# Products of v stored once and split when loaded, and the third slice's rounded weights kept in their tiles

## The chip, the cores and the metric

The kernel runs on one core of a Trainium2 chip. The core has four engines that matter here, each with its own queue of instructions worked off in order: TensorE (PE in the rows, with PEld for its weight loads), VectorE (DVE), ScalarE (ACT) and GpSimd (POOL); SP is a queue that only issues transfers, and GpSimd issues transfers too. What counts is the device time of one execution in microseconds (us), as the median of timed runs.

## The reference, cut to what matters

```
scores = einsum('bhij,hg->bgij', scale * q @ k.T, w_pre)   # heads mixed; 4 batches, 12 heads, 448 x 448
attn   = softmax(scores)
attn   = einsum('bhij,hg->bgij', attn, w_post)             # heads mixed again
x      = (attn @ v)  as [1792 tokens, 768]
h      = x @ w_in                                          # 768 -> 2048
out    = (max(h, 0) + alpha * min(h, 0)) @ w_out           # 2048 -> 768
```

All inputs of the second layer but alpha are drawn as 64-bit floats; w_in and w_out reach the chip so and are rounded to 32 bits there, with integer operations on VectorE (seven instructions for one half of a slice, see below).

## The kernel before

**Attention stage.** Work is cut into 16 chunks (4 batches, each with 120, 120, 120 and 90 queries) and these into groups of ten queries; two groups make one of 90 steps m. Per chunk: `qk` (L320, score products) and `qk_out` (L333, copies from PSUM into `st`, on ScalarE or VectorE); per group `relay` (L340, a transfer from `st` to `sr` that brings heads of one query side by side, RAHEAD = 3 steps early); per step `mix` (L347, first head mixing into `m`), `rmax` (L352, row maximum `nm` on VectorE), `exp` (L359, ScalarE), `norm` (L365 to L369, VectorE), `post` (L381, second head mixing into `pa`, 112 small matmuls) and `post_out` (L393, copies into `at`, on either engine). When a chunk is through, `pv` (L403) makes its products with v, x, in two halves hx; `pv_out` (L417, L419) splits each in a high part, rounded to TensorE's single-pass 32-bit type, and the low rest x - high; `store_x` (L424) stores both parts in HBM, in two transfers.

**Second stage.** x lies there as 4 blocks of 448 tokens (one batch each) and d_ff as 16 slices f of 128. A unit u is one block with one slice; the 64 units run in five groups of slices ([0,1,2], [3,4,5,6], [7,8,9], [10,11,12], [13,14,15]), within each over the blocks, forwards and backwards in turn. Of a unit, `l1` (L616) makes h = x w_in with 18 matmuls (high-high, high-low, low-high for six parts of 128), `act` (L629 to L635: t on ScalarE and VectorE, its high and low part g) the activation, and `l2` (L654) adds g w_out into six accumulators with 18 matmuls. TensorE's order is l1(u), l2(u-1), l1(u+1), ... After the last slice of a group the sums are taken out (`ao`, L664, L666). Three blocks of x lie in SBUF at a time; `prefetch` loads the next, six times in all, both parts (L518).

**Weights.** One half of a slice is w_in or w_out of one f. It is fetched (`cr`), rounded by seven VectorE operations (L60 to L68, the result in tile `ct`, of which there are two) and split into its high part on ScalarE (L546) and its low part on VectorE (L548), in tile `w`. The first three slices (NPRE = 3) are rounded during the attention stage, stored in HBM (`store_w`, L458), loaded again near its end (`load_pre`, L555) and split there. The other thirteen are rounded in the second stage by `convert2`, a generator that gives out one operation at a time against a budget: `conv_ops(0.8)` in the middle of a unit's activation and `conv_ops(3.4)` (0.6 after a group's last slice) at its end, a credit that runs up to 4.0 at most. Where the next unit's slice isn't ready, these lines force it ahead of l1:

```
while conv_at <= units[u][2] and units[u][2] >= NPRE:
    conv_ops(0.95)
l1(u)
```

**What sets the order.** Up to unit 1, `plan` sets it: a list of operations with engines, costs, due times (prio), predecessors and buffers (acq, rel), from which it takes at each moment the one that can start first, by start and due time; where an operation may run on ScalarE or VectorE it chooses. The names there are Q, S, L, M, R, E, N, P, A for the chain above, V, XH, XL, W for v's products, F, C, WS, LW, HH, HL for the weights, LX for x's loads, U and G for the first two units. Behind unit 1 the loop at the end of the kernel sets the order.

Of the kernel before, what the change touches and what calls it, by code (L numbers as in the profile page):

```python
# [21 lines left out]
NT = B * S  # L22
# [48 lines left out]
def plan(groups, first, chunk_list):  # L71
# [55 lines left out]
    for ci, (b, c) in enumerate(chunk_list):  # L127
        lb = (first[ci + 1] - 1) // 2
        mine = [("A",) + divmod(n, 2) for n in range(first[ci], first[ci + 1])]
        for hx in range(2):  # L130
# [3 lines left out]
            op(("XH", ci, hx), [act(0.8), dve(0.78)], pr, [("V", ci, hx)], (("xe", (ci, hx)),))  # L134
            op(("XL", ci, hx), dve(0.78), pr, [("XH", ci, hx)], rel=(("slot", (ci, hx, "v")),))
            for i in range(2):
                op(("W", ci, hx, i), dma(0.7), pr + 1, [("XL", ci, hx)], rel=(("xe", (ci, hx)),))
    nh = 2 * NPRE
    for i in range(nh):
# [8 lines left out]
        for k in range(2):  # L148
            op(("WS", i, k), dma(0.8), pr + 10 + k, [("C", i, 6)], rel=(("ct", i),))
    for bl in range(2):  # L150
        for i in range(2 * NCC):
            pr = NB - 10 + 6 * bl + i // 2
            op(("LX", bl, i), dma(0.95, 5.0), pr, [("LX", bl, -1), ("M", min(pr, NB - 1))])
        op(("LX", bl, -1), dma(0.0, 0.0), NB - 10 + 6 * bl, [("Q", NC - 1, 0)], (("st", ("x", bl)),))
    op(("OPEN",), dma(0.0, 0.0), NB - 9, [("Q", NC - 1, NP - 1), ("S", NC - 1, NP - 1)])
    for f in range(NPRE):
        for k in range(NWP):
            op(("LW", f, k), dma(0.8, 5.0), NB - 12 + 2 * f + k / 2, [("LW", f, -1)])
        op(("LW", f, -1), dma(0.0, 0.0), NB - 12 + 2 * f, [("WS", i, j) for i in range(nh) for j in range(2)], (("cr", ("w", f)),))
        for x in range(2):  # L160
            pr = NB - 3 + 1.2 * f + 0.6 * x
            before = [("OPEN",), ("V", NC - 2, 1)] + ([("HL", f, x - 1)] if x else [("HL", f - 1, 1)] if f else [])
            op(("HH", f, x), act(0.84), pr, [("LW", f, k) for k in range(NWP)] + before)
            op(("HL", f, x), dve(0.95), pr, [("HH", f, x)], rel=(("cr", ("w", f)),) if x else ())
    for u in range(2):
        op(("U", u), pe("U", "u"), NB + 2.5 + 2 * u, [("HL", u, 1), ("M", NB - 1)] + [("LX", 0, i) for i in range(2 * NCC)] + ([("V", NC - 1, 1)] if u else []),
# [58 lines left out]
def talking_heads_prelu(ctx: ExitStack, tc: tile.TileContext, q, k, v, w_pre, w_post, mask, w_in, w_out, alpha, out):  # L225
# [16 lines left out]
    x2 = dpool.tile([2, NCC, 128, NT], F32, name="x2")  # L242
    wsc = dpool.tile([NPRE, 128, 2 * DM], F32, name="wsc")
# [165 lines left out]
    def pv_out(ci, hx, part, eng):  # L409
        cn = CHUNKS[chunk_list[ci][1]][1]  # L410
        if part == 0:
            xe_t[ci, hx] = xep.tile([128, 2, 3, CW], F32R, tag="xe", name=f"xe{ci}_{hx}")
        xe, ps = xe_t[ci, hx], u_t["pv", ci, hx]
        hi, lo = (xe[:, i, :, :cn].rearrange("p c (k g) -> p c g k", k=GI) for i in range(2))
        src = ps[:, 0, :3 * CW].rearrange("p (c i) -> p c i", c=3)[:, :, :cn].rearrange("p c (g k) -> p c g k", k=GI)
        if part == 0:
# [4 lines left out]
    def store_x(ci, hx, i):  # L421
        b, c = chunk_list[ci]
        c0, cn = CHUNKS[c]
        nc.sync.dma_start(  # L424
            out=x2[i, 3 * hx:3 * hx + 3, :, b * S + c0:b * S + c0 + cn].rearrange("c p i -> p c i"),
            in_=xe_t[ci, hx][:, i, :, :cn].bitcast(F32))
# [33 lines left out]
    with tc.manual_schedule():  # L460
# [54 lines left out]
        def load_x(bl, i):  # L515
            open_x(bl, i)
            for t in range(2):
                nc.sync.dma_start(out=x_t[bl][:, t], in_=x2[t, :, :, bl * S:(bl + 1) * S].rearrange("c p i -> p c i"))  # L518

        def load_xp(bl, i, slot):  # L520
            if i < 0:
                open_x(bl, slot)
                return
            c, t = divmod(i, 2)
            nc.sync.dma_start(out=x_t[bl][:, t, c], in_=x2[t, c, :, bl * S:(bl + 1) * S])
# [148 lines left out]
        def split_pre(f, x, part):  # L674
            if x == 0 and part == 0:
                w_tile(f)
            split_w(f, x, wr[f][:, x * DM:(x + 1) * DM], part)
# [28 lines left out]
        def emit(n, e, got):  # L706
# [7 lines left out]
            elif kind in ("S", "A", "XH", "XL"):  # L714
# [108 lines left out]
```

## Time and profile before

| | |
|---|---|
| median of the timed runs | 854.63 us (853.2 to 855.88, 3 runs) |
| the profiled execution | 850.37 us, of which 848.6 us span |
| granted clock of TensorE, mean | 0.991 |
| busy: TensorE, weight loads, VectorE, ScalarE, GpSimd | 808.8, 665.0, 575.5, 341.3, 129.8 us |
| moved by DMA | 125.39 MB, mean 148 GB/s |

Busy time is the time in which an engine has an instruction running; the span runs from the first to the last instruction. A wait is told as the engine, the line that waited, the engine and line that ended the wait ("issue": nothing that the profile shows ended it), the total, the number and the longest. The attention stage ends at about 364 us, where unit 0 begins.

### The profile page before, as it was taken

How to read it: one execution, taken by the hardware profiler on the slowest of the kernel's cores; microseconds unless marked ns; L12 is line 12 of the kernel's file. 1: busy time of each engine (PE TensorE's matmuls, PEld its weight loads, DVE VectorE, ACT ScalarE, POOL GpSimd, SP SyncE). 2: the span in 40 equal slices, each digit the busy share in tenths (PEclk: the TensorE clock that was granted, in tenths of full speed). 3: DMA queues.
4: the chain of work that ended last, by engine and by line, in shares of the span. 5: the costliest groups of instructions: out<-in, count | busy, mean ns of one | idle time of the engine just before them, and what ended most of it. 6: DMA issues, size and time to landing. Idle time of an engine off the chain costs nothing.

```text
span 848.6 us, 24016 instructions
## 1 busy us (share of the span) xinstructions
PE 808.8 (95%) x10380; PEld 665.0 (78%) x10380; DVE 575.5 (68%) x1027; ACT 341.3 (40%) x715; POOL 129.8 (15%) x237
## 2 busy tenths in 40 slices
PE   8788998999898999889999999999999999999998
PEld 3455675677666777689999999989999899999997
DVE  5669787999697978675666877248773967763323
ACT  4657766776566775532322221112212212121111
POOL 4443324343242221000000000000000000000000
PEclk9999999999999999999999999999999999999999
DMA  8698878887897679777221431002510242104113
GB/s 214 185 205 253 222 205 215 238 241 219 208 241 204 205 220 283 235 188 284 75 75 37 148 133 40 36 0 84 196 46 29 74 168 75 38 1 172 48 48 124
DMA packets 75374, 125.39 MB, mean 148 GB/s; under 512 B 33876, under 2 KB 64020, under 8 KB 75268
## 3 DMA queue, kind: packets, MB, share of 16 engines
q1 hardware_dynamic: 58228, 64.78, 25.1%
q0 software_dynamic: 16560, 58.01, 24.0%
q8 instruction: 82, 1.34, 0.7%
q10 hardware_dynamic: 480, 1.06, 0.5%
q14 instruction: 24, 0.20, 0.1%
HBM read 66.16 MB, written 18.92 MB: 100 GB/s over the span
## 4 chain that ended last, share of the span: by engine, by line
PE 87%; DMA 5%; DVE 4%; issue 2%; ACT 2%; SPq 0%; POOL 0%; ACTq 0%; DVEq 0%
PE acc L654 27%; PE h L616 27%; PE x L403 9%; PE pa L381 9%; PE m L347 7%; PE s L320 7%; DMA cr<-in_w_in_dram 2%; DMA sr<-st 1%; ACT e L359 1%; DVE nm L352 1%; DMA k<-in_k_dram 1%; DVE at L393 1%; DMA x<-xe 1%; DMA q<-in_q_dram 0%; DVE ao L666 0%
## 5 line engine op out<-in xcount | busy, mean ns | idle before, releaser
L654 PE MATMUL acc<-g,w 128*128 128x448 f32 x1152 | 245.7, 366 | 3.3 <-DVE g L635 2.0
L616 PE MATMUL h<-x,w 128*128 128x448 f32 x1152 | 248.3, 368 | 0.0
L654 PEld LDWEIGHTS acc<-g,w 128*128 128x128 f32 x1152 | 216.0, 188 | 23.3 <-DVE g L635 2.8
L616 PEld LDWEIGHTS h<-x,w 128*128 128x128 f32 x1152 | 216.1, 188 | 21.2
L381 PEld LDWEIGHTS pa<-r,e 64*64 64x64 f32 x5040 | 107.3, 134 | 57.5 <-issue 36.1
L631 DVE SCALAR_TENSOR_TENSOR t<-t,oma,h 128x448 f32<-128x448 f32 x64 | 43.5, 680 | 156.7 <-ACT t L629 156.7
L629 ACT ACTIVATE t<-h 128x448 f32<-128x448 f32 x64 | 34.9, 545 | 271.3 <-PE h L616 271.3
L381 PE MATMUL pa<-r,e 64*64 64x60 f32 x5040 | 108.7, 221 | 18.5 <-issue 13.2
L359 ACT ACTIVATE e<-m,nm 128x448 f32<-128x448 f32 x180 | 113.3, 641 | 23.6 <-DVE nm L352 13.5
L352 DVE TENSOR_REDUCE nm<-m 128x2 f32<-128x896 f32 x90 | 97.3, 1085 | 14.6 <-PE m L347 14.0
L320 PE MATMUL s<-k,q 64*64 64x448 f32 (+2 forms) x768 | 96.7, 556 | 4.8 <-ACT e L359 1.5
L347 PE MATMUL m<-sr,wk 64*64 64x448 f32 x720 | 93.4, 560 | 6.0 <-DMA sr<-st 3.6
L403 PEld LDWEIGHTS x<-at,v 128*64 128x64 f32 x1536 | 77.6, 141 | 19.8 <-ACT e L359 5.8
L403 PE MATMUL x<-at,v 128*64 128x120 f32 (+1 forms) x1536 | 84.5, 268 | 2.2 <-DVE s L366 0.8
L340 POOL DMA_DIRECT2D sr<-st x90 | 54.9, 611 | 200.8 <-PE m L347 148.6
L393 ACT COPY at<-pa 128x480 f32<-128x480 f32 x95 | 53.8, 575 | 53.4 <-PE pa L381 50.8
L333 ACT COPY st<-s 120x896 f32<-120x896 f32 (+1 forms) x68 | 61.5, 912 | 27.8 <-PE s L320 24.3
L393 DVE COPY at<-pa 128x480 f32<-128x480 f32 x85 | 55.0, 652 | 17.9 <-PE pa L381 16.3
L633 ACT CAST g<-t 128x448 fp32r<-128x448 f32 x64 | 36.3, 567 | 51.1 <-DVE t L631 51.1
L666 DVE TENSOR_TENSOR ao<-ao,acc 128x448 f32<-128x448 f32 x96 | 52.7, 613 | 1.7 <-PE acc L654 1.7
L320 PEld LDWEIGHTS s<-k,q 64*64 64x64 f32 (+2 forms) x768 | 29.9, 131 | 28.8 <-issue 10.4
L635 DVE TENSOR_TENSOR g<-t,g 128x448 fp32r<-128x448 f32 x64 | 39.8, 622 | 16.2 <-ACT g L633 16.2
(51 smaller groups left out, 523.3 us busy)
## 6 DMA issues: line engine op xcount, KB each, us to landing
sr<-st SPq DMA_DIRECT2D x90, 210.0 KB
sr<-st POOLq DMA_DIRECT2D x90, 210.0 KB, 5.5
x<-x SPq DMA_DIRECT2D x12, 1344.0 KB
cr<-in_w_in_dram POOLq DMA_DIRECT2D x13, 768.0 KB, 4.7
cr<-in_w_out_dram POOLq DMA_DIRECT2D x13, 768.0 KB, 4.5
x<-xe SPq DMA_DIRECT2D x48, 180.0 KB
x<-x SPq DMA_DIRECT2D x24, 224.0 KB
out_dram<-ao SPq DMA_DIRECT2D x24, 224.0 KB
```

The source lines that it names most:

```text
L320: nc.tensor.matmul(ps[i0:i1, hf, :S], q_t[ci][r, p * cn + i0:p * cn + i1], k_t[b, p // 2][r, p % 2, :], start=True, stop=True)
L333: copy(dst[:cn, p], u_t.pop(("qk", ci, p))[:cn, :, :S])
L340: dma.dma_start(out=sr_t[n][SR0:SR0 + GP], in_=s_t[ci][r:CHUNKS[chunk_list[ci][1]][1]:CHUNKS[chunk_list[ci][1]][1] // GI])
L347: nc.tensor.matmul(ps[hf:hf + 64, u, :S], wk[r, :], g[r, :], start=True, stop=True)
L352: nc.vector.tensor_reduce(out=nm, in_=m_t[m][:, :, :S], axis=AX.X, op=ALU.max, negate=True)
L359: nc.scalar.activation(out=e_t[m][:, u], in_=m_t[m][:, u, :S], func=AF.Exp, bias=nm_t[m][:, u:u + 1], scale=1.0, accum_out=se_t[m][:, u:u ...
L381: nc.tensor.matmul(dst[:, :, HI * u:HI * u + HI], e[h, u, 64 * jb:64 * jb + 64], r[h, u].rearrange("p (h i) -> p h i", h=H), start=True, s ...
L393: copy_on[eng](dst, pa[g][:, :NS * GP].rearrange("p (s i) -> p s i", i=GI))
L403: nc.tensor.matmul(ps[64 * t:64 * t + 64, 0, cl * CW:cl * CW + cn], v_t[b, hx][:, s, (2 * cl + t) * D:(2 * cl + t + 1) * D], a_t[ci][:, s, ...
L616: nc.tensor.matmul(ps[:, :S], w[:, tw, cc * 128:(cc + 1) * 128], x[:, tx, cc, :], start=(i == 0), stop=(i == 3 * NCC - 1))
L654: nc.tensor.matmul(accs[c][:, :S], w[:, tw, c * 128:(c + 1) * 128], g[:, tg], start=(f == fs[0] and i == 0), stop=(f == fs[-1] and i == 2))
L666: nc.vector.tensor_tensor(acc_sb[c, bl], acc_sb[c, bl], accs[c][:, :S], ALU.add)
```

## The change

Two things change, and the planner draws up the order anew from its altered list.

1. v's products are copied once from PSUM (one copy per half chunk, X, in place of XH and XL) and stored once as 32-bit floats. A loaded block of x comes as one transfer (per part c for blocks 0 and 1) into what was the place of the low parts, and is then split in six parts: the high part on ScalarE, and x - high on VectorE, in place. For blocks 0 and 1 the splits XA and XB are operations of the plan; for later loads `splits_x` puts three into each of the two units after the load's, and their cost is taken off the budget of `conv_ops`.
2. The rounded halves of the third slice (f = 2) stay in their two `ct` tiles until they are split. Their four stores and four loads go. The split of f = 0 is due earlier, and no longer waits for the last chunk but one.

```
+            op(("X", ci, hx), [act(0.8), dve(0.78)], pr, [("V", ci, hx)], (("xe", (ci, hx)),), (("slot", (ci, hx, "v")),))
+            op(("W", ci, hx), dma(0.7), pr + 1, [("X", ci, hx)], rel=(("xe", (ci, hx)),))
...
+            if i < nh - 2:
+                op(("WS", i, k), dma(0.8), pr + 10 + k, [("C", i, 6)], rel=(("ct", i),))
...
+        for c in range(NCC):
+            pr = NB - 10 + 6 * bl + c
+            op(("LX", bl, c), dma(0.95, 5.0), pr, [("LX", bl, -1), ("M", min(pr, NB - 1))])
+            ps_ = NB - 4 + 0.5 * c + (9 if bl else 0)
+            op(("XA", bl, c), act(0.57), ps_, [("LX", bl, c)])
+            op(("XB", bl, c), dve(0.65), ps_, [("XA", bl, c)])
...
+        kept = f == NPRE - 1
+            pr = (NB - 3 if f else NB - 8) + 1.2 * f + 0.6 * x
+            before = [("OPEN",)] + ([("V", NC - 2, 1)] if f else []) + ([("HL", f, x - 1)] if x else [("HL", f - 1, 1)] if f else [])
+            op(("HH", f, x), act(0.84), pr, before if kept else [("LW", f, k) for k in range(NWP)] + before)
...
+    def pv_out(ci, hx, eng):
         cn = CHUNKS[chunk_list[ci][1]][1]
+        xe_t[ci, hx] = xep.tile([128, 3, CW], F32, tag="xe", name=f"xe{ci}_{hx}")
+        ps = u_t.pop(("pv", ci, hx))
         src = ps[:, 0, :3 * CW].rearrange("p (c i) -> p c i", c=3)[:, :, :cn].rearrange("p c (g k) -> p c g k", k=GI)
-        if part == 0:
-            copy_on[eng](hi, src)
-        else:
-            nc.vector.tensor_tensor(lo, src, hi, ALU.subtract)
+        copy_on[eng](xe_t[ci, hx][:, :, :cn].rearrange("p c (k g) -> p c g k", k=GI), src)
...
+        def split_x(bl, c, part):
+            hi, x = x_t[bl][:, 0, c].bitcast(F32R), x_t[bl][:, 1, c]
+            if part == 0:
+                nc.scalar.copy(hi, x)
+            else:
+                nc.vector.tensor_tensor(x.bitcast(F32R), x, hi, ALU.subtract)
...
+        x_todo = []
+
+        def splits_x(u):
+            n = 0
+            while x_todo and x_todo[0][0] <= u:
+                _, bl, c = x_todo.pop(0)
+                split_x(bl, c, 0)
+                split_x(bl, c, 1)
+                n += 1
+            return 0.65 * n
...
                     load_x(bl, free[0])
+                    x_todo.extend((u + 1 + c // 3, bl, c) for c in range(NCC))
...
             if u < nu:
-                conv_ops(0.6 if units[u - 1][2] == FGROUPS[units[u - 1][0]][-1] else 3.4)
+                conv_ops((0.6 if units[u - 1][2] == FGROUPS[units[u - 1][0]][-1] else 3.4) - splits_x(u))
```

VectorE in the middle of the attention stage, where the second half (hx = 1) of the seventh chunk's products is taken out (`xe`; `m`, `nm`, `s`, `r` are a step's mixed scores, maxima, sums and weights, `at` and `ct` as above), before:

```order
L365 TENSOR_SCALAR s_2997<-se_2979 128x2
L366 RECIPROCAL s_2997<-s_2997 128x2
L369 TENSOR_TENSOR r_3000<-wq,s_2997 128x120
L419 TENSOR_TENSOR xe_1_2995<-x_1_2945,xe_1_2995 128x3x12x10
L393 COPY at_3039<-pa_114 128x48x10
L352 TENSOR_REDUCE nm_3047<-m_2989 128x2
```

The subtraction that makes the low part stands ahead of the copy of `pa` and of the next maximum. The same engine at the same place of the changed program (lines 5 higher):

```order
L370 TENSOR_SCALAR s_2972<-se_2954 128x2
L371 RECIPROCAL s_2972<-s_2972 128x2
L374 TENSOR_TENSOR r_2975<-wq,s_2972 128x120
L63 TENSOR_SCALAR ct_1_2959<-cr_1_2527 128x768
L357 TENSOR_REDUCE nm_3009<-m_2967 128x2
L398 COPY at_3018<-pa_114 128x48x10
```

There is no such row any more; both halves are copied by ScalarE here, and a rounding operation and the maximum follow directly.

VectorE in the second stage, from unit 13's g to unit 14's g and on, before (`w_7128` is slice 6, first used in unit 15; `t` and `g` are a unit's activation and its low part):

```order
L68 TENSOR_TENSOR ct_0_7057<-ct_0_7057,ce_0_7012 128x768
L60 TENSOR_SCALAR ce_1_7130<-cr_1_7009 128x768
L548 TENSOR_TENSOR w_7128<-ct_0_7057,w_7128 128x768
L631 SCALAR_TENSOR_TENSOR t_7170<-t_7170,oma,h_7133 128x448
L635 TENSOR_TENSOR g_7171<-t_7170,g_7171 128x448
L63 TENSOR_SCALAR ct_1_7176<-cr_1_7009 128x768
```

Slice 6's first half (w_in) is split ahead of unit 14's t, its second half follows behind unit 14's g. After the change (lines 4 higher; `w_7000` is slice 5, `w_7132` slice 6):

```order
L552 TENSOR_TENSOR w_7000<-ct_1_7066,w_7000 128x768
L635 SCALAR_TENSOR_TENSOR t_7117<-t_7117,oma,h_7080 128x448
L63 TENSOR_SCALAR ct_0_7122<-cr_0_6998 128x768
L639 TENSOR_TENSOR g_7118<-t_7117,g_7118 128x448
L64 TENSOR_SCALAR ce_0_7077<-ce_0_7077 128x768
L65 SCALAR_TENSOR_TENSOR ct_0_7122<-cr_0_6998,ct_0_7122 128x768
L66 TENSOR_SCALAR ce_0_7077<-ce_0_7077 128x768
L67 SCALAR_TENSOR_TENSOR ce_0_7077<-cr_0_6998,ce_0_7077 128x768
L68 TENSOR_TENSOR ct_0_7122<-ct_0_7122,ce_0_7077 128x768
L60 TENSOR_SCALAR ce_1_7134<-cr_1_7074 128x768
L552 TENSOR_TENSOR w_7132<-ct_0_7122,w_7132 128x768
L63 TENSOR_SCALAR ct_1_7137<-cr_1_7074 128x768
```

Now slice 5's second half stands where slice 6's first half stood, and both halves of slice 6 (the first is shown, the second begins in the last row) stand between unit 14's g and unit 15's t.

## Rows read from the trace of the kernel before

**Rows 1.** The page: busy tenths of TensorE, VectorE, ScalarE in 40 equal slices

```profile
PE   8788998999898999889999999999999999999998
...
DVE  5669787999697978675666877248773967763323
ACT  4657766776566775532322221112212212121111
```

**Rows 2.** The page: shares by engine of the chain that ended last

```profile
PE 87%; DMA 5%; DVE 4%; issue 2%; ACT 2%; SPq 0%; POOL 0%; ACTq 0%; DVEq 0%
```

**Rows 3.** Groups to 364 us: operation, shapes, count | busy, mean ns | idle before

```profile
L393 DVE COPY at<-pa 128x480 f32<-128x480 f32 x84 | 54.3, 652 | 17.9 <-PE pa L381 16.3 <-ACT st L333 0.6 <-issue 0.2
...
L333 DVE COPY st<-s 120x896 f32<-120x896 f32 (+1 forms) x28 | 30.3, 1085 | 14.5 <-PE s L320 13.6 <-DMA sr<-st 0.6
...
L419 DVE TENSOR_TENSOR xe<-x,xe 128x360 fp32r<-128x360 f32 (+1 forms) x29 | 22.3, 771 | 4.0 <-ACT xe L417 3.3 <-DMA x<-xe 0.4
...
L417 DVE CAST xe<-x 128x360 fp32r<-128x360 f32 (+1 forms) x12 | 9.4, 785 | 5.3 <-PE x L403 5.3
```

**Rows 4.** Waits to 364 us: total us, times, longest us

```profile
ACT e L359 <- DVE nm L352: 13.5, 11, 3.0
PE pa L381 <- issue: 13.2, 9, 3.5
...
PE m L347 <- DMA sr<-st: 3.6, 4, 1.4
```

**Rows 5.** The row maxima, all and from 160 to 200 us: first and last start

```profile
L352 DVE TENSOR_REDUCE nm<-m x90: 1073/1083/1093, 20.1 to 357.3; 128x2 f32<-128x896 f32 x90
...
L352 DVE TENSOR_REDUCE nm<-m x12: 1079/1083/1093, 160.7 to 197.7; 128x2 f32<-128x896 f32 x12
```

**Rows 6.** Windows: length, busy us by engine, then granted clock, DMA share, GB/s

```profile
36.00:39.00 3.00, 2.91 (x87) 1.89 (x91) 2.37 (x6) 1.89 (x6) 0.66 (x2) 1.00 0.05 16
...
223.00:224.00 1.00, 1.00 (x23) 0.70 (x22) 0.00 (x0) 0.46 (x1) 0.00 (x0) 0.50 0.56 192
...
219.00:231.00 12.00, 8.46 (x196) 6.34 (x188) 7.38 (x14) 6.36 (x16) 3.37 (x6) 0.86 0.72 198
```

**Rows 7.** Timeline of TensorE: start, us, instructions [idle before, what ended it]

```profile
36.09 0.38 PE L381 MATMUL pa<-r,e 64*64 64x60 f32 x10 [2.31 <-issue]
...
222.78 0.79 PE L381 MATMUL pa<-r,e 64*64 64x60 f32 x18 [3.54 <-issue]
...
350.82 0.38 PE L381 MATMUL pa<-r,e 64*64 64x60 f32 x10 [1.78 <-issue]
```

**Rows 8.** Groups from 364 us on, columns as in rows 3

```profile
L635 DVE TENSOR_TENSOR g<-t,g 128x448 fp32r<-128x448 f32 x64 | 39.8, 622 | 16.2 <-ACT g L633 16.2
...
L419 DVE TENSOR_TENSOR xe<-x,xe 128x270 fp32r<-128x270 f32 (+1 forms) x3 | 2.1, 709 | 1.1 <-ACT xe L417 1.1
```

**Rows 9.** Waits from 364 us on, columns as in rows 4

```profile
DVE t L631 <- ACT t L629: 156.7, 58, 5.5
...
PE acc L654 <- DVE t L631: 1.3, 1, 1.3
```

**Rows 10.** Timeline in unit 14: TensorE's products and VectorE's operations between them

```profile
473.13 3.83 PE L654 MATMUL acc<-g,w 128*128 128x448 f32 x18
...
475.28 0.62 DVE L635 TENSOR_TENSOR g<-t,g 128x448 fp32r<-128x448 f32 x1 [0.63 <-ACT g L633]
475.82 0.55 DVE L63 TENSOR_SCALAR ct<-cr 128x768 int32<-128x768 int32 x1
476.29 0.55 DVE L64 TENSOR_SCALAR ce<-ce 128x768 int32<-128x768 int32 x1
...
476.80 3.88 PE L616 MATMUL h<-x,w 128*128 128x448 f32 x18
...
480.52 3.81 PE L654 MATMUL acc<-g,w 128*128 128x448 f32 x18
...
481.07 0.96 DVE L548 TENSOR_TENSOR w<-ct,w 128x768 fp32r<-128x768 f32 x1 [0.31 <-ACT w L546]
```

More of the change, by code (lines that the diff above doesn't have):

```diff
@@ L156, in plan @@
     for f in range(NPRE):
-        for k in range(NWP):
-            op(("LW", f, k), dma(0.8, 5.0), NB - 12 + 2 * f + k / 2, [("LW", f, -1)])
-        op(("LW", f, -1), dma(0.0, 0.0), NB - 12 + 2 * f, [("WS", i, j) for i in range(nh) for j in range(2)], (("cr", ("w", f)),))
+        kept = f == NPRE - 1
+        if not kept:
+            for k in range(NWP):
+                op(("LW", f, k), dma(0.8, 5.0), NB - 12 + 2 * f + k / 2, [("LW", f, -1)])
+            op(("LW", f, -1), dma(0.0, 0.0), NB - 12 + 2 * f, [("WS", i, j) for i in range(nh - 2) for j in range(2)] + [("C", nh - 1, 6)],
+               (("cr", ("w", f)),))
         for x in range(2):
[L161 to L164, printed above, removed]
+            pr = (NB - 3 if f else NB - 8) + 1.2 * f + 0.6 * x
+            before = [("OPEN",)] + ([("V", NC - 2, 1)] if f else []) + ([("HL", f, x - 1)] if x else [("HL", f - 1, 1)] if f else [])
+            op(("HH", f, x), act(0.84), pr, before if kept else [("LW", f, k) for k in range(NWP)] + before)
+            op(("HL", f, x), dve(0.95), pr, [("HH", f, x)], rel=(("ct", 2 * f + x),) if kept else (("cr", ("w", f)),) if x else ())
     for u in range(2):
-        op(("U", u), pe("U", "u"), NB + 2.5 + 2 * u, [("HL", u, 1), ("M", NB - 1)] + [("LX", 0, i) for i in range(2 * NCC)] + ([("V", NC - 1, 1)] if u else []),
+        op(("U", u), pe("U", "u"), NB + 2.5 + 2 * u, [("HL", u, 1), ("M", NB - 1)] + [("XB", 0, c) for c in range(NCC)] + ([("V", NC - 1, 1)] if u else []),
            (("slot", ("u", u)),))
@@ L407, in talking_heads_prelu, with store_x @@
     xe_t = {}
[L409 removed]
+    def pv_out(ci, hx, eng):
         cn = CHUNKS[chunk_list[ci][1]][1]
[L411 to L414 removed]
+        xe_t[ci, hx] = xep.tile([128, 3, CW], F32, tag="xe", name=f"xe{ci}_{hx}")
+        ps = u_t.pop(("pv", ci, hx))
         src = ps[:, 0, :3 * CW].rearrange("p (c i) -> p c i", c=3)[:, :, :cn].rearrange("p c (g k) -> p c g k", k=GI)
[L416 to L421 removed]
+        copy_on[eng](xe_t[ci, hx][:, :, :cn].rearrange("p c (k g) -> p c g k", k=GI), src)
+    def store_x(ci, hx):
         b, c = chunk_list[ci]
         c0, cn = CHUNKS[c]
[L424 to L426 removed]
+        nc.sync.dma_start(out=x2[3 * hx:3 * hx + 3, :, b * S + c0:b * S + c0 + cn].rearrange("c p i -> p c i"),
+                          in_=xe_t.pop((ci, hx))[:, :, :cn])
     def fetch_w(f, x):
@@ L516, in load_x, with load_xp @@
             open_x(bl, i)
[L517 to L521, printed above, removed]
+            nc.sync.dma_start(out=x_t[bl][:, 1], in_=x2[:, :, bl * S:(bl + 1) * S].rearrange("c p i -> p c i"))
+        def load_xp(bl, c, slot):
+            if c < 0:
                 open_x(bl, slot)
                 return
-            c, t = divmod(i, 2)
-            nc.sync.dma_start(out=x_t[bl][:, t, c], in_=x2[t, c, :, bl * S:(bl + 1) * S])
+            nc.sync.dma_start(out=x_t[bl][:, 1, c], in_=x2[c, :, bl * S:(bl + 1) * S])
+        def split_x(bl, c, part):
[4 more added lines that the diff above has]
+                nc.vector.tensor_tensor(x.bitcast(F32R), x, hi, ALU.subtract)
         def w_tile(f):
@@ L676, in split_pre @@
                 w_tile(f)
-            split_w(f, x, wr[f][:, x * DM:(x + 1) * DM], part)
+            split_w(f, x, wr[f][:, x * DM:(x + 1) * DM] if f in wr else conv[2 * f + x][0].bitcast(F32), part)
         def turn():
@@ L713, in emit @@
                     s_t[a[0]] = s_tile(got["st"], f"st{a[0]}")
[L714 to L716 removed]
+            elif kind in ("S", "A", "X"):
+                {"S": qk_out, "A": post_out, "X": pv_out}[kind](*a, e)
             elif kind == "L":
```

16 lines of the change are left out of this document (3 added, 13 removed).

## Prediction

> **What bounds the kernel now.** I read the busy tenths first [rows 1]: TensorE stands at 7 to 9 in the first seventeen slices (the attention stage, up to about 364 us) and at 9 after them, VectorE at 5 to 9 in the first and mostly at 2 to 8 in the second part. The chain that ended last says the same: 87% of it is TensorE [rows 2]. So a microsecond counts only where TensorE waits, and the two stages differ. In the second stage (64 units, each a first product of 18 matmuls and a second of 18) a unit takes 480.52 - 473.13 = 7.39 us [rows 10] and TensorE hardly stops: one wait of 1.3 us for VectorE stands at its very start [rows 9]. The attention stage is looser. Its clock is the row maximum, one for each of 90 steps: from 160.7 to 197.7 us twelve of them take (197.7 - 160.7) / 11 = 3.36 us each, over the whole stage (357.3 - 20.1) / 89 = 3.79 us [rows 5]. So TensorE can go 0.43 us a step faster than it does on average, 38 us over 89 steps, and it is not at its floor. What holds it is partly VectorE and ScalarE handing work to each other (exp waits 13.5 us for the maxima) and partly gaps in which TensorE's sequencer waits for nothing shown, 13.2 us in nine places before the head-mixing products L381 [rows 4]; four of these are of 1.8 to 3.5 us (the first, the longest and the last in [rows 7]).
>
> **The attention stage: VectorE is relieved.** The order of the two programs gives the counts, the trace the durations. Removed are the 32 low parts L419: 29 of 22.3 us [rows 3] and three of 2.1 us [rows 8], 24.4 us. In their place x is split after loading. The trace has no such in-place split; its nearest row, from below and above alike, is L635, a 128x448 subtraction of the same kind and output type, 0.622 us [rows 8]. Twelve of them (blocks 0 and 1) stand before the second unit: +7.5 us. The planner also shares out the copies anew: score copies on VectorE go from 28 to 34 (6 x 1.085 = +6.5), first copies of v's products from 13 to 9 (4 x 0.785 = -3.1), head-mixing copies from 85 to 83 (2 x 0.652 = -1.3), by [rows 3]. VectorE's net is -24.4 + 7.5 + 6.5 - 3.1 - 1.3 = -14.8 us. (The splitting as such isn't reduced: blocks are loaded eight times, so 48 splits follow 32; it is moved to where VectorE has time.)
>
> How much of the 14.8 us reaches the end is the disputed term. Its ends are 0, if TensorE takes the whole stage anyway, and 14.8. I stand near the upper end, because a step has 0.43 us of room and the relief is 14.8 / 90 = 0.16 of it. But where a sequencer gap falls, VectorE has caught up and a relieved VectorE brings nothing: four of the sixteen query chunks hold a gap of 1.8 us or more [rows 7], so I take 14.8 x 12/16 = **-11.1 us**. Below nothing it can't go from this alone, since nothing is added to TensorE.
>
> ScalarE gets twelve splits and loses some copies; it stands at 4 to 7 tenths in the stage [rows 1], which hides that. The transfers that go (32 of 64 stores of v's products, 12 of 24 early and 6 of 12 late loads, 4 stores and 4 loads of f = 2's weights) leave SP's queue, with the relays behind them. TensorE waited 3.6 us for relays in the whole stage [rows 4], so quicker ones give 0 to 3.6 us; I count nothing, since there were only four such waits. A new wait: ScalarE and VectorE now take block 0's loads at the head of their queues, with the exps and maxima of the last steps behind. In SP's order each load stands several relays ahead of its split, so I price it at nothing; a late load would cost its lateness, us for us. The two f = 2 halves kept in their rounding tiles block nobody: the next user of those tiles starts in unit 2.
>
> **The turn.** Unit 0's second product waited 1.3 us for VectorE [rows 9]. In the new order unit 0's activation is done before the last v products run: **-1.3 us**, or 0.
>
> **The second stage: a unit that comes too late.** 36 splits (six loads, 36 x 0.622 = 22.4 us on VectorE) lie beside TensorE: VectorE idles 156.7 us before L631 there [rows 9]. But they are paid out of the budget that paces the rounding of the later weights, 1.95 us of 3.4 in units 2 to 5, 7.8 us in all, and a half of f's weights takes 482.03 - 475.82 = 6.2 us to round and split [rows 10]. So rounding falls more than one half behind, and the code forces it where a weight is due. In the order, f = 6 (first used in unit 15) had its first half split before unit 14's activation; now both halves stand between unit 14's g and unit 15's t. The trace has the same sequence for one half: g starts at 475.28, L64 at 476.29, w is done at 481.07 + 0.96 = 482.03 [rows 10]. Without the 0.47 us of L63 (now ahead of g), w_in is ready 482.03 - 475.28 - 0.47 = 6.28 us after g starts, and g starts 475.28 - 473.13 = 2.15 us after the second product before it; a 0.12 us lateness from the half before comes on top: 8.55 us. Unit 15's first product would have started after 476.80 - 473.13 = 3.67 us. TensorE stands still for 8.55 - 3.67 = **+4.9 us**. The other half (6.2 us) then lies under that product and the next two. Bounds: 4.5 (two matmuls need the high part only) and 5.
>
> After a gap TensorE's clock can fall. After 3.54 us of gap at 222.78 the granted clock was 0.50 (the lower of its two levels, 1.2 GHz against 2.4) and 0.86 on average over 219 to 231 us, a loss of 12 x 0.14 = 1.7 us; after 2.31 us of gap at 36.09 it stayed at 1.00 [rows 6, 7]. The coming gap is longer than either, in a stage where TensorE sets the end: **+1.7 us**, bounds 0 and 3.4 (twice the row's loss). The Trainium skill speaks against the change here: TensorE: Matmul & The Clock Gate, section "Why this matters for your kernels", says that an idle gap between bursts of matmuls sends the clock back to half. The gap at 222.78 agrees with it, that at 36.09 does not. By the rule the sum is as I give it; by the row at 36.09 it is 1.7 us lower.
>
> **Sum.** -11.1 - 1.3 + 4.9 + 1.7 = -5.8 us. The profiled execution took 850.37 us (span 848.6) and would take 844.6. It lies 4.3 us below the median of the timed runs, 854.63, from which I count: 854.6 - 5.8 = **848.8 us**.
>
> **Rivals.** Let g be the attention stage's gain; the time is then 854.6 + 5.3 - g.
> 1. TensorE already sets the attention stage's end (slower). For it: TensorE's 8 and 9 tenths [rows 1]; a matmul shown as busy may hide no wait at all. Against: 3.36 against 3.79 us a step [rows 5]. At g = 0 it gives 859.9; it decides from g under 5.3, measurably under 2.7 (857.2).
> 2. Half a gain. The relief arrives only where VectorE was late for a maximum. g between 2.7 and 7.9: 852.0 to 857.2, no change that shows.
> 3. Unit 15 does not wait, because TensorE is late there for another reason. Then +4.9 and +1.7 go: 854.6 - 12.4 = 842.2. Against: the order is fixed, the durations are nearly constant, and VectorE waits for TensorE in nearly every unit before (58 times [rows 9]), so it can't be ahead.
> 4. The sequencer gaps shrink with the transfers. If they come from busy DMA, the three in [rows 7] (2.31 + 3.54 + 1.78 = 7.6 us) might go, and the sum with them: 841.2. Against: nothing in the trace ties the gaps to transfers.
>
> **How the numbers follow.** A difference under 0.3% (2.6 us) can't be told from none. My forecast, g from 7.9 to 14.8 with the wait at unit 15, covers 845.1 to 852.0, chance 0.52. Rival 1 (below 2.7) 0.12, rival 2 0.16, rival 3 0.12, rival 4 0.08. Faster: 0.52 + 0.12 + 0.08 = 0.72; same 0.16; slower 0.12. The range leaves out rivals 1 and 4, 0.20 in all: 842.0 to 857.2.
>
> **What will show it.** Steps: the last maximum at about 346 us instead of 357.3, and L635's fellow for x at 0.62 us; a g well below 7.9 with VectorE less busy means rival 2 or 1. Turn: no wait of the first second product. Unit 15: one wait of a first product (L620 after) for VectorE's w of 4.5 to 5 us, some 110 us after the stage's start, and a granted clock of 0.5 for about 3 us behind it; no such row means rival 3. The issue waits of L381's fellow: 13 us again, or rival 4. I am wrong beyond all this if a load of block 0 comes late and holds ScalarE before U0, or if the 36 splits stand in front of an activation that TensorE is waiting for.

## The result, and the profile after

The changed kernel takes 842.25 us (median of four runs, 841.81 to 845.22), the kernel before beside it 855.25 us; the ratio is 0.9855, with a 95% interval of 0.9821 to 0.9889. So it is faster, by 12.4 us (9.5 to 15.3 by the interval), where 5.8 us had been forecast. Measured twice more beside other runs, on two chips, it came to 0.9935 (0.9901 to 0.9968) and 0.9815 (0.9761 to 0.9869). Weighted by their runs the three ratios give 0.9886, about 10 us: the sign is sure, the size is not sharp. Ratios here compare the executions in the faster of two states alone (three of 1121 to 1585 us, one of e6 and two of e8 with the profiled one, are thus left out), so they are not always the quotient of the medians. A single execution of either kernel often strays by 4 us, and at times by 8, so the profiled pair (850.37 us before, 845.22 us after) shows mechanisms better than sums.

The page of after: engines' busy time, then VectorE's busy tenths in 40 equal slices, then what the DMA queues moved. Lines have moved by a few numbers: the head-mixing products are L386 (L381 before), the products with v L408 (L403), the first and second products of a unit L620 and L658 (L616 and L654).

```profile
PE 807.4 (96%) x10380; PEld 668.3 (79%) x10380; DVE 581.3 (69%) x1043; ACT 359.7 (43%) x763; POOL 130.1 (15%) x237
...
DVE  4659897888789877766667877448675966674423
...
DMA packets 54989, 107.26 MB, mean 127 GB/s; under 512 B 20660, under 2 KB 43636, under 8 KB 54884
```

The same line of the page of before:

```profile
DMA packets 75374, 125.39 MB, mean 148 GB/s; under 512 B 33876, under 2 KB 64020, under 8 KB 75268
```

18.1 MB and 20,385 packets are gone. VectorE's tenths have not fallen by much in the attention stage [rows 1]: it does the same steps in a shorter time. The stage's clock, the 90 row maxima (count, duration least, median and most, first and last start):

```profile
L357 DVE TENSOR_REDUCE nm<-m x90: 1077/1085/1093, 20.5 to 344.6; 128x2 f32<-128x896 f32 x90
```

The last starts 12.7 us earlier than before [rows 5]; the forecast was "about 346". TensorE's waits up to 345 us (total, times, longest):

```profile
PE pa L386 <- issue: 9.1, 8, 3.1
PE m L352 <- DMA sr<-st: 4.8, 4, 2.3
PE x L408 <- issue: 4.4, 1, 4.4
PE m L352 <- issue: 2.2, 2, 1.2
```

The gaps behind nothing shown are 9.1 + 4.4 + 2.2 = 15.7 us in all, about as much as before: there the 13.2 us of [rows 4] and three more, up to 364 us, make 16.2.

```profile
PE s L320 <- issue: 1.2, 1, 1.2
PE m L347 <- issue: 1.1, 1, 1.1
...
PE x L403 <- issue: 0.7, 1, 0.7
```

Then the turn and unit 15, on TensorE's timeline (start, length, instructions, idle before and what ended it):

```profile
360.48 3.92 PE L620 MATMUL h<-x,w 128*128 128x448 f32 x18
365.75 3.92 PE L658 MATMUL acc<-g,w 128*128 128x448 f32 x18 [1.35 <-DVE t L635]
...
461.85 3.83 PE L658 MATMUL acc<-g,w 128*128 128x448 f32 x18
469.46 6.59 PE L620 MATMUL h<-x,w 128*128 128x448 f32 x18 [3.78 <-ACT w L550]
475.89 0.37 PE L658 MATMUL acc<-g,w 128*128 128x448 f32 x1
```

Of the same stretch, VectorE's low part of w and the weight loads of unit 15's first product:

```profile
469.44 0.96 DVE L552 TENSOR_TENSOR w<-ct,w 128x768 fp32r<-128x768 f32 x1 [0.30 <-ACT w L550]
...
470.45 5.22 PEld L620 LDWEIGHTS h<-x,w 128*128 128x128 f32 x16 [0.49 <-DVE w L552]
```

The wait of the first second product is still there, as long as before [rows 9]. Unit 15 does wait for its weights: for ScalarE's high part, with which two matmuls can start, and then the other 16 for VectorE's low part, until 470.40 us. Its first product takes 6.59 us instead of 3.88 [rows 10], for that second wait lies in it, and the clock is low, as the windows show (length, busy us by engine, then granted clock, DMA share, GB/s):

```profile
468.00:470.00 2.00, 0.54 (x2) 0.50 (x2) 1.66 (x3) 0.83 (x1) 0.37 (x1) 0.55 0.44 95
470.00:472.00 2.00, 2.00 (x6) 1.43 (x5) 2.00 (x4) 0.00 (x0) 0.00 (x0) 0.50 0.74 298
472.00:474.00 2.00, 2.00 (x7) 1.76 (x7) 1.93 (x4) 0.00 (x0) 0.03 (x1) 0.50 0.00 0
474.00:476.00 2.00, 2.00 (x9) 1.84 (x8) 1.66 (x3) 0.83 (x1) 0.49 (x1) 0.74 0.52 98
```

The clock stands at its lower level, 1.2 GHz, until about 475 us. From one second product to the next it is 475.89 - 461.85 = 14.04 us instead of 7.39 [rows 10]: 6.65 us lost, where the prediction had 4.9 + 1.7 = 6.6.

So the second stage went as forecast, and the first stage paid more than forecast. The experiments ask what paid.

### The profile page after: what moved, and what is told of

Same layout as the page of the kernel before. It is cut to its first block, busy times and chain, and to the rows that moved or that the text cites. A ratio compares the mean times of both kernels' runs of the same rounds, so it can differ in the third digit from the quotient of the medians.

```text
span 843.3 us, 24014 instructions
## 1 busy us (share of the span) xinstructions
PE 807.4 (96%) x10380; PEld 668.3 (79%) x10380; DVE 581.3 (69%) x1043; ACT 359.7 (43%) x763; POOL 130.1 (15%) x237
## 4 chain that ended last, share of the span: by engine, by line
PE 88%; DVE 5%; DMA 3%; issue 2%; ACT 2%; SPq 0%; ACTq 0%; DVEq 0%
PE h L620 27%; PE acc L658 27%; PE x L408 10%; PE pa L386 9%; PE m L352 8%; PE s L325 7%; DMA sr<-st 1%; DVE nm L357 1%; DMA k<-in_k_dram 1%; ACT e L364 1%; DVE w L552 1%; DMA q<-in_q_dram 0%; DVE at L398 0%; DVE st L338 0%; DVE ao L670 0%
## 5 line engine op out<-in xcount | busy, mean ns | idle before, releaser
L620 PE MATMUL h<-x,w 128*128 128x448 f32 x1152 | 250.9, 371 | 3.8 <-ACT w L550 3.8
L658 PE MATMUL acc<-g,w 128*128 128x448 f32 x1152 | 245.8, 366 | 2.5 <-DVE t L635 1.4
L620 PEld LDWEIGHTS h<-x,w 128*128 128x128 f32 x1152 | 218.0, 190 | 26.0 <-ACT w L550 4.2
L658 PEld LDWEIGHTS acc<-g,w 128*128 128x128 f32 x1152 | 216.0, 188 | 22.6 <-DVE g L639 1.9
L386 PEld LDWEIGHTS pa<-r,e 64*64 64x64 f32 x5040 | 108.6, 135 | 45.7 <-issue 33.4
L386 PE MATMUL pa<-r,e 64*64 64x60 f32 x5040 | 107.8, 222 | 9.3 <-issue 9.1
L357 DVE TENSOR_REDUCE nm<-m 128x2 f32<-128x896 f32 x90 | 97.6, 1087 | 22.6 <-PE m L352 21.7
L408 PEld LDWEIGHTS x<-at,v 128*64 128x64 f32 x1536 | 76.4, 139 | 18.9 <-issue 7.2
L408 PE MATMUL x<-at,v 128*64 128x120 f32 (+1 forms) x1536 | 83.1, 266 | 5.4 <-issue 4.4
L338 ACT COPY st<-s 120x896 f32<-120x896 f32 (+1 forms) x62 | 56.1, 913 | 23.2 <-PE s L325 21.9
L352 PEld LDWEIGHTS m<-sr,wk 64*64 64x64 f32 (+1 forms) x720 | 27.4, 135 | 29.7 <-issue 21.0
```

Source lines behind the costliest of these rows:

```text
L338: copy(dst[:cn, p], u_t.pop(("qk", ci, p))[:cn, :, :S])
L352: nc.tensor.matmul(ps[hf:hf + 64, u, :S], wk[r, :], g[r, :], start=True, stop=True)
L357: nc.vector.tensor_reduce(out=nm, in_=m_t[m][:, :, :S], axis=AX.X, op=ALU.max, negate=True)
L386: nc.tensor.matmul(dst[:, :, HI * u:HI * u + HI], e[h, u, 64 * jb:64 * jb + 64], r[h, u].rearrange("p (h i) -> p h i", h=H), start=True, s ...
L408: nc.tensor.matmul(ps[64 * t:64 * t + 64, 0, cl * CW:cl * CW + cn], v_t[b, hx][:, s, (2 * cl + t) * D:(2 * cl + t + 1) * D], a_t[ci][:, s, ...
L620: nc.tensor.matmul(ps[:, :S], w[:, tw, cc * 128:(cc + 1) * 128], x[:, tx, cc, :], start=(i == 0), stop=(i == 3 * NCC - 1))
```

## The experiments

All runs stand beside runs of the kernel before on their chip: 854.59 us for the first four, 853.67 us for the next four, 855.86 us for the last four. "The base" is the changed kernel.

| kernel | median us | ratio to before, 95% interval |
|---|---|---|
| e1: splits not charged to the rounding | 835.78 | 0.981 (0.9759 to 0.986) |
| e2: only the split of x moved | 840.42 | 0.9847 (0.98 to 0.9894) |
| e4: subtractions back, planned | 846.37 | 0.9915 (0.9882 to 0.9948) |
| e5: transfers back, planned | 847.21 | 0.9944 (0.9905 to 0.9984) |
| e6: the changed kernel again | 847.85 | 0.9935 (0.9901 to 0.9968) |
| e7: transfers doubled, same order | 852.87 | 1.0005 (0.9974 to 1.0035) |
| e8: as many transfers, hardly any bytes | 847.17 | 0.9945 (0.991 to 0.9979) |
| e3: only the third f's weights kept | 848.71 | 0.9944 (0.9915 to 0.9973) |
| e12: the changed kernel a third time | 840.82 | 0.9815 (0.9761 to 0.9869) |
| e11: subtractions back, same order | 846.27 | 0.9888 (0.9844 to 0.9932) |
| e13: e7 and e11 together | 851.30 | 0.9984 (0.9948 to 1.0021) |
| e10: only x moved, splits not charged | 832.55 | 0.9725 (0.968 to 0.9769) |

### The wait at unit 15 (e1)

```diff
-                conv_ops((0.6 if units[u - 1][2] == FGROUPS[units[u - 1][0]][-1] else 3.4) - splits_x(u))
+                splits_x(u)
+                conv_ops(0.6 if units[u - 1][2] == FGROUPS[units[u - 1][0]][-1] else 3.4)
```

> The changed kernel, with the splits of later blocks no longer taken off the budget of the rounding operations (nothing else changes up to unit 1). Theory: in unit 15 TensorE stood 3.8 us for slice 6's weights and then 6.8 us at half clock, 6.65 us in all; with the budget kept, slice 6's first half is split a unit earlier, as before the change, and this goes: 842.25 - 6.6 = 835.6 us, and no wait of a first product for w in the trace. Rival: the rounding is late for another reason, or the six splits now lying on top of the rounding hold up activations in units 2 to 5: 842 us or more.

835.78 us, 6.5 us under the base as first measured. In its trace TensorE's waits from 330 us on are these, all that there are:

```profile
PE pa L386 <- issue: 4.2, 2, 2.8
PE acc L658 <- DVE g L639: 2.0, 2, 1.0
PE acc L658 <- DVE t L635: 1.4, 1, 1.4
PE x L408 <- DVE at L398: 0.9, 1, 0.9
```

No first product waits for w any more. From the first second product to the end it takes 830.6 - 358.91 = 471.7 us; the base took 843.3 - 365.75 = 477.6, the kernel before 848.6 - 377.03 = 471.6. The 6 us at unit 15 come from the budget alone, and the splits themselves cost the second stage nothing. This is shown, the more so as the stretch behind the first second product hardly varies: in the six traces of the base's order with the budget charged (the base's three, e7, e11, e13) it takes 476.7 to 477.6 us. What differs between executions lies ahead of it.

### Which half of the change pays (e2, e3)

e2 is the changed kernel with the third f's weights stored and loaded again and the split of f = 0 due as before; e3 is the kernel before with only that part of the change. The core of e2:

```diff
-            if i < nh - 2:
-                op(("WS", i, k), dma(0.8), pr + 10 + k, [("C", i, 6)], rel=(("ct", i),))
+            op(("WS", i, k), dma(0.8), pr + 10 + k, [("C", i, 6)], rel=(("ct", i),))
...
-        kept = f == NPRE - 1
+        kept = False
```

> Only v's products stored once and split when loaded; slice 2's rounded weights stored, loaded and split as before the change. Theory that VectorE's relief in the attention stage carries the gain: nearly all of it stays, 842 to 845 us, with the same wait in unit 15. Rival, that the earlier and lighter turn between the stages carries it (slice 2 kept, slice 0 split early): about half, 848 to 850 us.

840.42 us: the move of the split carries the whole gain, and nothing shows that the third f's part adds to it.

> The kernel before with one part of the change: the third f's weights kept in their rounding tiles; v's products are split and stored in two as before. With the run that had only the split moved (840.42 us, the whole gain) the rest should be nothing: 852 to 857 us. If the prediction's turn term is real, or four stores and four loads of weights count, 850 to 853 us.

848.71 us against 853.67: alone, in the old order, the third f's part gains 5.0 us (2.3 to 7.3 by the interval), more than either range expected. The two halves do not add, and the turn shows one reason. The first second product of the base starts behind a wait of 1.35 us for VectorE's t (shown above). That of e2, and that of e3:

```profile
360.92 4.22 PE L657 MATMUL acc<-g,w 128*128 128x448 f32 x18
```

```profile
372.98 1.38 PE L658 MATMUL acc<-g,w 128*128 128x448 f32 x6
...
375.07 2.70 PE L658 MATMUL acc<-g,w 128*128 128x448 f32 x12 [0.71 <-DVE t L635]
```

Either half alone shortens the wait for VectorE's t, to some 0.3 us in e2 (4.22 us instead of 3.92) and to 0.71 in e3, behind six matmuls. The whole 1.35 us stands in all eight traces with the changed kernel's order (the base's three, e1, e7, e8, e11, e13). It belongs to that order and not to the two halves as such: e4 and e5 below have both halves in other orders, and their first second products take 3.88 and 4.21 us with no wait ahead. From the last row maximum to this product it takes 377.03 - 357.3 = 19.7 us before, 365.75 - 344.6 = 21.2 in the base, 360.92 - 341.8 = 19.1 in e2. So the turn became 1.4 us longer, not 1.3 shorter.

### VectorE or transfers, with a new plan (e4, e5)

e4 gives VectorE the 32 subtractions back, but neither stores nor loads their result; e5 gives the stores and loads back without the subtractions. Both tell the planner. The cores of the two edits:

```diff
+            op(("XD", ci, hx), dve(0.78), pr, [("X", ci, hx)], rel=(("slot", (ci, hx, "v")),))
...
+        if eng is None:
+            nc.vector.tensor_tensor(lo, src, hi, ALU.subtract)
```

```diff
-            op(("W", ci, hx), dma(0.7), pr + 1, [("X", ci, hx)], rel=(("xe", (ci, hx)),))
+            for i in range(2):
+                op(("W", ci, hx, i), dma(0.7), pr + 1, [("X", ci, hx)], rel=(("xe", (ci, hx)),))
...
+            for t in range(2):
+                nc.sync.dma_start(out=x_t[bl][:, t, c], in_=x2[t, c, :, bl * S:(bl + 1) * S])
```

> The changed kernel with the 32 subtractions of the low part made again on VectorE in the attention stage (planned like before, holding PSUM as long as before; the result isn't used, the stores and loads stay halved). Theory VectorE: the attention stage's gain is given back, 11 us or more, 853 to 858 us (24 us of VectorE work are back, and the splits after loading stay). Rival, fewer transfers: the gain stays, 842 to 846 us.

> The changed kernel with the transfers of v's products as before: each half chunk is stored twice (to two places, the same data) and both places are loaded. VectorE's work is that of the changed kernel. Theory VectorE: the gain stays, 842 to 845 us. Rival, fewer transfers (fewer late instruction blocks on TensorE, quicker relays): half of the gain or more is given back, 848 to 855 us, with more gaps that nothing shown ends.

846.37 and 847.21 us: each lies between the two theories' numbers, e4 0.4 us above its rival's end, and e5 close to its rival's (by its ratio, 849.8 us, inside), but without the additional gaps that this rival expected: 15.3 us of them up to 380 us, the base 15.7. Neither VectorE nor the transfers are the whole, and since the planner lays out another order each time, the order is mixed in. The next runs leave the order alone.

### The transfers, in the changed kernel's own order (e6, e7, e8)

e7 issues each store of v's products and each early load twice on SP, without telling the planner; e8 does the same with second transfers of one partition.

```diff
-        nc.sync.dma_start(out=x2[3 * hx:3 * hx + 3, :, b * S + c0:b * S + c0 + cn].rearrange("c p i -> p c i"),
-                          in_=xe_t.pop((ci, hx))[:, :, :cn])
+        for i in range(2):
+            nc.sync.dma_start(out=x2[i, 3 * hx:3 * hx + 3, :, b * S + c0:b * S + c0 + cn].rearrange("c p i -> p c i"),
+                              in_=xe_t[ci, hx][:, :, :cn])
...
-            nc.sync.dma_start(out=x_t[bl][:, 1, c], in_=x2[c, :, bl * S:(bl + 1) * S])
+            for t in range(2):
+                nc.sync.dma_start(out=x_t[bl][:, 1 - t, c], in_=x2[t, c, :, bl * S:(bl + 1) * S])
```

> The changed kernel once more, unedited, as the base of the three runs beside it on the same chip. So far it stood at 842.25 us (841.81 to 845.22) in four runs. Every theory expects 840 to 845 us.

> The changed kernel in which each of the 32 stores of v's products, and each of the twelve early loads, is issued twice on SP, the second time to and from a second DRAM area; the planner isn't told, so that the order on TensorE, VectorE, ScalarE and POOL stays word for word that of the changed kernel, and VectorE's work too. The result is the same as before. Theory T (in the attention stage it is the transfers themselves that the change took away, bytes on the DMA engines or entries on SP's queue): 4 to 8 us of the gain are lost, 846 to 850 us, the late steps (78 and on) come about 8 us later. Theory O (what the run with the transfers given back lost came from its planner laying out another order): no loss, 840 to 845 us.

> As the run with the doubled stores and loads and the changed kernel's own order, but each second transfer moves one partition out of 128: as many entries on SP's queue, hardly any bytes. If the bytes on the DMA engines are what costs: as the changed kernel, 840 to 845 us. If the place on SP's queue costs (the relays stand behind it): as the run with whole second transfers, 846 to 850 us.

Against e6's 847.85 us on the same chip (a little above what was expected of it), e7 takes 852.87, 5.0 us more, and no longer differs from the kernel before (1.0005); e8 takes 847.17, as the base. So theory T holds, and it is the data moved, not the places on SP's queue. (Bytes and packets go together here: a second transfer of one partition in 128 has hardly any of either, so the runs don't tell which of the two costs; below, "the bytes" stands for both.) What they were, on the page of e7:

```profile
DMA packets 69517, 115.54 MB, mean 136 GB/s; under 512 B 33652, under 2 KB 58164, under 8 KB 69412
```

8.3 MB and 14,528 packets more than the base cost 5.0 us, with some 3 us of scatter either way, though no engine computes anything for them. They cost it nearly all ahead of the turn: from the last maximum to the first second product e7 takes 21.7 us, the base's three executions 21.0 to 21.2. The other sign, late steps some 8 us later, is not so large: e7's last maximum starts at 347.6 us, the base's at 344.6, 341.7 and 345.2. Where they cost it, a single trace says only in part. TensorE's waits up to 345 us in e7:

```profile
PE pa L386 <- issue: 12.4, 10, 2.5
PE x L408 <- issue: 5.8, 2, 3.6
PE m L352 <- DMA sr<-st: 3.8, 2, 3.3
...
PE m L352 <- issue: 1.5, 2, 1.2
```

The waits for relays are no longer than in the base (3.8 against 4.8 us); the gaps of the sequencer are 19.7 us, the most of any trace, where the base's three executions show 15.7, 12.4 and 16.7. But e13, with the same bytes, shows 12.1. That the bytes cost through these gaps is therefore not shown.

### VectorE's time, in the changed kernel's own order (e11, e12, e13)

```diff
+        hi, lo = (xe_t[ci, hx][:, i, :, :cn].rearrange("p c (k g) -> p c g k", k=GI) for i in range(2))
+        nc.vector.tensor_tensor(lo, hi, hi, ALU.subtract)
```

> The changed kernel unedited, as the base on this chip. It stood at 842.25 us in four runs and at 847.85 us in eleven on another chip, with the kernel before at 854 to 855 us both times. Every theory expects 841 to 849 us, and the ratio to the kernel before between 0.985 and 0.994.

> The changed kernel with one 128x3x120 subtraction on VectorE ahead of each of the 32 stores of v's products, of the size that was removed, its result read by nobody; the order on TensorE, ScalarE, POOL and SP is word for word that of the changed kernel. About 24 us of VectorE's time come back. Theory V (the prediction's: 12/16 of VectorE's time reaches the end): 18 us above the base. Theory B (VectorE's time reaches the end only in a few places, the bytes carry more): 1 to 5 us above the base, as the planned return of the subtractions gave.

846.27 us against e12's 840.82 (just under what was expected of it): 5.5 us for some 24 us of VectorE's work, 0.23 us for each, not 0.75. The size is rough, since e12's six executions run from 834.99 to 849.44 us: by this scatter the cost lies between nearly nothing and 11 or 12 us. Theory V, with 18, falls. VectorE's groups up to 345 us show where the rest went (busy us, mean ns, then idle before and what ended it); first the row maxima of the base, then of e11 with the new operation:

```profile
L357 DVE TENSOR_REDUCE nm<-m 128x2 f32<-128x896 f32 x90 | 97.6, 1087 | 22.6 <-PE m L352 21.7
```

```profile
L357 DVE TENSOR_REDUCE nm<-m 128x2 f32<-128x896 f32 x89 | 96.2, 1084 | 11.9 <-PE m L352 11.5
...
L425 DVE TENSOR_TENSOR xe<-xe 128x360 f32<-128x360 f32 (+1 forms) x28 | 21.7, 776 | 4.3 <-ACT xe L419 4.2
```

In the base VectorE idles 22.6 us ahead of its maxima, nearly all of it for TensorE's mixes (21.0 and 23.8 in its other two executions); in e11 11.9, in e13 14.0. The 21.7 us of subtractions filled 10.7 us of idle time there, and 3.1 us ahead of the score copies (18.1 in the base, 15.0 in e11). So an engine that waits for TensorE before its own critical operation has room, and what it is relieved of goes in part into that room instead of moving the end. In the kernel before the same row showed less room, 12.5 us:

```profile
L352 DVE TENSOR_REDUCE nm<-m 128x2 f32<-128x896 f32 x87 | 94.0, 1085 | 12.5 <-PE m L347 12.1
```

e13 puts e7's and e11's edits together.

> The changed kernel's order with both: the subtractions of the last run and the doubled stores and early loads. All the work that the split's move took out of the attention stage is back, in the changed kernel's own order. If the two costs add up (6 us for the transfers, 1 to 5 us for VectorE): 7 to 11 us above the base, the kernel before's time. If they hide behind each other: 5 to 7 us above the base. If the changed kernel's order is itself worth something: clearly below the kernel before.

851.30 us, 10.5 above the base: 5.0 + 5.5, so the two costs add up and do not hide behind each other. The bytes are the surer part: beside e11 they cost 5.0 us once more, while 5.5 and 10.5 both rest on e12's six executions. But e13 is no slower than the kernel before (0.9984, 0.9948 to 1.0021), although it also carries the 6 us at unit 15 and twelve splits that the kernel before does not have there. So the rest of the change is worth about 6 us plus 0.16% of 855, some 7 us (4 to 10 by the interval). It holds the planner's new order of the attention stage, the PSUM space of a half chunk's products, which is free after one copy now (e13's subtractions read SBUF), and the third f's weights kept. Which of these it is stays open. The kept weights can hardly be it: where they are undone (e2, e10, each in an order of its own), nothing is lost.

### A better version (e10)

> A version meant to be faster than both: only the split of x is moved (the third f's weights stored and loaded as before), and the second stage's splits of x don't draw on the rounding's budget. By the runs with each alone: no wait of a first product for w in unit 15, some 6 us below the base: 0.975 to 0.985 of the kernel before. If the third f's part gains by itself, as it did alone in the kernel before, it comes out 3 to 5 us above the uncharged version, at the base.

The edits are those of e1 and e2 together. 832.55 us, 0.9725 of the kernel before: the fastest of all, a little below the 0.975 to 0.985 expected, and 3.2 us under e1 (on another chip, with intervals that overlap). The end of its turn, and units around the fifteenth:

```profile
355.77 4.22 PE L657 MATMUL acc<-g,w 128*128 128x448 f32 x18
...
463.21 3.88 PE L619 MATMUL h<-x,w 128*128 128x448 f32 x18
...
470.60 3.88 PE L619 MATMUL h<-x,w 128*128 128x448 f32 x18
```

No wait stands ahead of the first second product (0.3 us lies in it: 4.22 us instead of 3.92), and the units pass at 470.60 - 463.21 = 7.39 us without a stop. So beside the moved split the kept weights bring no gain that shows.

## Why the prediction was right, and where it was not

The sign and the range held; the forecast of 848.8 us lies above the 842.25 us measured, and near the second measurement's 0.9935 (849.7 us of 855.25). That the range held is in part luck: 842.25 us lies 0.25 us above its lower end, and below the 845.1 to 852.0 us that the forecast's own mechanism covered. The range reached down so far for the third rival, no wait at unit 15, which did not come true. In the prediction's formula, 854.6 + 5.3 - g, the measured time is a g of 17.7 us, and the three ratios together one of 15.0: above the 14.8 that was its upper end. Step by step:

- **Unit 15, +4.9 and +1.7: right.** The row came where it was forecast, and e1 took the whole away. w was whole at 469.44 + 0.96 = 470.40 us, 8.55 us after the second product's start at 461.85, as worked out. The wait shown is 3.78 us because two matmuls need the high part only, which the bound of 4.5 had allowed for: the other 16 start at 470.45, where without a wait they would have started at 461.85 + 3.67 + 2/18 x 3.72 = 465.93 (3.72 is 480.52 - 476.80 [rows 10]), so 4.5 us late. Of the 6.65 us lost some 2.1 us are left for the clock, beside 1.7 (an estimate); it stood low until about 475 us, for some 5.5 us of products and not 3.
- **The turn, -1.3: wrong in sign.** The wait stayed and the turn grew by 1.4 us. The prediction took unit 0's activation for what the product waits on; the wait ends at unit 1's t (it stands behind all 18 matmuls of unit 1's first product). The likely reason is that the accumulators take over the PSUM space of unit 1's h; this was not tried. e2 and e3 show that the order decides it.
- **VectorE, -14.8 x 12/16 = -11.1: the factor failed.** The net count was sound (the same groups of after give -13), and the subtraction that splits x took 0.62 us as forecast, but e11 prices VectorE's time at 5.5 / 24 = 0.23 of it, at most about half by the scatter. Of 14.8 us 0.23 leaves 3.4. The mistake: I read "0.43 us of room a step" as room that VectorE alone could release, and left out the 12.5 us in which VectorE itself waited for TensorE's mixes.
- **Transfers, "I count nothing": the step that failed most.** Its bound, 0 to 3.6 us, came from the four relay waits of TensorE; e7 measures 5.0 us for 8.3 MB of such transfers, and e13 beside e11 5.0 again, above the bound's end. Bytes can cost without a row that names them as the releaser.
- **The planner's order: not in the sum at all.** e13 leaves about 7 us for it and what comes with it, the size of the whole forecast.

By these runs the gain is 5.5 for the subtractions, 5.0 for the bytes, about 7 for the order (the longer turn and the twelve new splits already in it), less 6 at unit 15: some 11 to 12 us, beside 10 by the three ratios. The order's share is what the others leave over, so that this sum is no test of itself. The forecast's -11.1 for the stage met the profiled stretch up to the first second product (365.75 against 377.03, -11.3) by luck: the profiled execution of before lay 4.9 us under its median, that of after 3.0 above its own.

Of the rivals, the first and second (no gain or half a gain in the stage) are out by the result: even 0.9968, the smallest gain that the three intervals allow, makes g 8.0. The third is out by the row at unit 15. The fourth, gaps that shrink with the transfers, is half right: less traffic was worth 5 us, but the gaps of the base are about as long as before (15.7 us and 16.2).

## What to carry to other kernels

When a change takes bytes away from a stage whose DMA engines are eight tenths busy, price them by doubling them in the unchanged order rather than by the waits that name a transfer: here 8.3 MB cost 5 us that no wait row showed to be theirs. A busy engine that waits for the bounding engine ahead of its own critical operation gives back only a fraction of what is taken off it, about a quarter here and hardly more than half. And work that is moved into a paced stage should not be paid from the budget of other paced work that has a due time: uncharging it was worth 6 us, more than the forecast's net gain.

## What the runs showed of the hardware

The gaps in which TensorE's sequencer waits for nothing shown stand at fixed distances in its instruction stream. Three of after, on its timeline, and the counts of matmuls and weight loads between the first two (x behind the first two busy times of the window):

```profile
57.26 1.06 PE L408 MATMUL x<-at,v 128*64 128x120 f32 x8 [4.40 <-issue]
...
219.74 0.59 PE L386 MATMUL pa<-r,e 64*64 64x60 f32 x12 [3.05 <-issue]
...
337.24 0.50 PE L386 MATMUL pa<-r,e 64*64 64x60 f32 x17 [2.38 <-issue]
```

```profile
57.10:219.60 162.50, 156.00 (x3930) 111.93 (x3930) 132.75 (x266) 111.79 (x262) 59.22 (x106) 0.98 0.79 217
```

Between the two largest gaps of before [rows 7]:

```profile
36.00:222.50 186.50, 171.99 (x4304) 117.61 (x4305) 156.02 (x314) 128.67 (x298) 69.37 (x124) 1.00 0.84 222
```

7860 instructions are 31 times 253.5, 8609 are 34 times 253.2. The same places recur in the other runs with the changed order: counted from the start, gaps of 0.6 us or more stand behind 1195, 4996, 9309 and 15,142 of these instructions in the base's three executions and in e1 alike. Which of the places cost 1 us and which 4 changes from execution to execution. The Trainium skill, Runtime: NRT & Kernel Launch, section "Instruction fetch mechanics", says that instructions are fetched in blocks of 256 while the block before runs, and that the crossing is mostly hidden. The spacing agrees with the blocks, if a few instructions of each are not in these counts. "Mostly hidden" agrees in number, with 11 such waits where some 55 of these distances lie between the 1195th and the 15,142nd instruction; but the 11 cost 15.7 us of the attention stage. That the fetch is what the sequencer waits for is argued from the spacing, not shown.

After such gaps the clock can fall to its lower level, but the length of the gap does not decide it. Windows of after, behind the gap of 3.05 us and then behind that of 2.38 us:

```profile
219.70:222.00 2.30, 2.27 (x26) 1.59 (x29) 0.00 (x0) 1.54 (x5) 0.00 (x0) 0.50 0.51 173
222.00:226.00 4.00, 4.00 (x130) 2.88 (x124) 3.54 (x7) 2.56 (x7) 2.61 (x5) 0.94 0.58 153
337.20:339.00 1.80, 1.76 (x46) 1.10 (x48) 1.20 (x3) 1.25 (x4) 0.00 (x0) 0.86 1.00 321
339.00:341.00 2.00, 2.00 (x53) 1.54 (x51) 1.01 (x4) 1.22 (x4) 0.00 (x0) 0.50 0.73 269
```

A gap of before, on its timeline and in its window, and one of e1:

```profile
262.56 0.34 PE L381 MATMUL pa<-r,e 64*64 64x60 f32 x6 [2.21 <-issue]
...
264.00:266.00 2.00, 2.00 (x22) 2.00 (x22) 1.93 (x6) 2.00 (x5) 0.00 (x0) 0.50 1.01 233
```

```profile
330.63 0.50 PE L386 MATMUL pa<-r,e 64*64 64x60 f32 x17 [2.84 <-issue]
...
331.00:335.00 4.00, 3.60 (x118) 2.32 (x109) 3.63 (x8) 3.76 (x9) 0.00 (x0) 1.00 0.52 191
```

Behind 2.21 and 2.38 us it fell to 0.50, behind 2.84 us it stayed at 1.00, as it did before behind 2.31 us [rows 6, 7]. The Trainium skill, TensorE: Matmul & The Clock Gate, section "Why this matters for your kernels", says that an idle gap between bursts of matmuls, when it is long enough, sends the clock back to half. (The prediction left the condition out; so its gap of 2.31 us is no case against the Trainium skill.) The gap of 3.05 us and the wait of 3.78 us at unit 15 agree; the four shorter ones, of which two fell and two did not, are not told apart by their length. These gaps, and the clock behind them, fall differently in each execution: two executions of the same order, the base's and e1's, reach the last maximum at 344.6 and 337.7 us. Their gaps up to 345 us come to nearly as much (15.7 and 15.0 us); their granted clock from 20 to 337.7 us is 0.97 and 0.99, and 0.02 of 317.7 us is some 6 us, an estimate from figures of two digits. That the clock behind the gaps makes much of the scatter from run to run is therefore likely, not shown.
